# A key list for four engines and the transfers written anew, in a linear-attention and mixture-of-experts kernel

## The chip, the cores and the metric

One core of a Trainium2 chip runs one launch of the program. Its engines are TensorE (PE; its weight loads are shown as PEld), VectorE (DVE), ScalarE (ACT), GpSimd (POOL) and SyncE (SP), which issues nearly all transfers. The metric is the device time of one execution in microseconds, median of several runs.

## The reference

For each of 4 batches and 8 heads a complex state runs over 768 steps; then 3072 tokens go through two of eight experts each:

```python
mag = np.sqrt(a_re * a_re + a_im * a_im)
scale = np.minimum(mag, 0.999) / (mag + 1e-06)      # a_re_n, a_im_n = a * scale
for t in range(S):
    new_re = ar * S_re - ai * S_im
    new_im = ar * S_im + ai * S_re
    kv = np.einsum('bhd,bhe->bhde', k[:, :, t], v[:, :, t])
    S_re, S_im = (new_re + kv, new_im)
    y[:, :, t] = np.einsum('bhd,bhde->bhe', q[:, :, t], S_re)
logits = x @ w_gate
noisy_logits = logits + np.log1p(np.exp(x @ w_noise)) * noise
top2 = np.argpartition(-noisy_logits, 2, axis=1)[:, :2]       # softmax over the two
h = np.maximum(x[mask] @ w1[e], 0.0)
out[mask] += top2_w[mask, k, None] * (h @ w2[e])
```

## The kernel before, in words

The attention is cut into 24 units of 128 steps (n = 0 to 23; four units, one a batch, make a group g = n // 4; two units make a pair m). For a pair, `p1` (L330 on) turns the decay into logarithms (keys A1 to A4, D1 to D4), `p2a`, `p2carry` and `p2t` (L352 to L378) take the angle, add the carry of the group before (D5, which reads the tile `car`), sum along the steps on PE (P1, then A6, D7), and send the last row back to `car` by a transfer (S7). `p3` (L387) does the same for the magnitudes (P2, A9, A10, D9), sends a row to DRAM and back as a column (S5, S6). D10 and D11 turn q and k, PE transposes them (P3, P4; copied by A11, A12), forms scores (P5, masked by D12), the state (P6, D13) and the output (P7, A13; turned by P8, A14). After each group, the gate (keys G0 to G12; the last two groups in two parts, as G0.4 and G0.4b) picks experts and slots; POOL scatters the rows to `xs` in DRAM (`gate_scatter`, L566).

The experts follow: 72 matmuls of the first layer of expert 0, for the first 320 slots, are laid into the last attention units (P22.000 to P22.007, L764), then the second layer (P23.00 to P23.02, L833 and L839) and the first layer of expert 1. The remaining slots of expert 0 need every scatter: `xgb` is loaded from `xs` (L623) and turned on PE (`x_T`, L738). From there on the experts run one after another, outside the order given by hand.

What sets the order: a string of 1270 keys, `ORDER` (L208). A key's letter names the engine (A, D, P, S; G keys by the table `ON`, else DVE), and `key` (L289) collects the instructions made under it; most keys are one instruction, S6 (L399), S9 (L350), S14 and D25 are two, S10.0 four transfers. The keys' places also set where each step is emitted (`PLACE`, L862). The loop at L989 to L992 then chains, for each engine, the first instruction of a key behind the last one of the key before it. Of a key with two transfers, only the first has a floor and only the second holds what follows. Where no chain binds, the planner behind the tile framework places an instruction by its own costs. `PACE` (L527) holds back single scatters until a named ACT key is done.

Of the kernel before, what the change touches and what calls it, by code (L numbers as in the profile page):

```python
# [77 lines left out]
def kernel(  # L78
# [127 lines left out]
    phases, K = {}, {}  # L206

    ORDER = """  # L208
        A0.0 S1a.0 S1.1 S2a.0 S2.1 S1b.0 S2b.0 S3.0 A1a.0 A2a.0 A1b.1 A1a.1 D1a.0 A2b.1 A2a.1 D2a.0 S11.0
# [9 lines left out]
        D12a.1 S6.3 A6.7 P5b.1 D7.6 S1.5 A12.2 D7.7 P7a.1 S3.7 D8.3 P8.0 S7.5 A8.3 S12.5 P5a.2 D13.2 A7.3
        D11.3 P3.3 A14.0 D12b.1 A0.4 P2.4 D4.3 P5b.2 A9.4 D12a.2 P7b.1 A11.3 S5.4 D12b.2 P2.5 S2.5 A10.4 S4.4  # L220
        P4.3 A13.1 D9.4 S7.6 A9.5 S3.8 P2.6 A1.4 S6.4 D11.4 P7a.2 A10.5 S1.6 P7b.2 A12.3 D10.4 S5.5 P2.7 D9.5
        A13.2 P3.4 S4.5 A9.6 A2.4 S12.6 D10.5 P5a.3 A11.4 S3.9 D1.4 P5b.3 S7.7 A1.5 D12a.3 P4.4 A10.6 D12b.3
        A2.5 P7a.3 S6.5 D2.4 P7b.3 A12.4 P6.3 S2.6 D16.0 D1.5 S1.7 A13.3 P5a.4 S12.7 D13.3 A9.7 S5.6 A3.4 D2.5
        P8.1 P3.5 S3.10 A10.7 D3.4 S4.6 A3.5 P5b.4 D12a.4 A14.1 A4.4 D3.5 P7a.4 A11.5 D4.4 G0.0 A4.5 D11.5
        P6.4 S5.7 G1.0 S6.6 D9.6 A0.5 P8.2 P8.3 D12b.4 P4.5 S3.11 A14.2 D10.6 A5.4 S4.7 P7b.4 A14.3 S11.6 D5.4
        A5.5 S8.4 S12.8 D4.5 A12.5 P1.8 S2.7 P1.9 D5.5 A6.8 P3.6 A13.4 D7.8 S4.8 A6.9 D13.4 S6.7 G2.0 A11.6
        D7.9 S9.4 G3.0 D11.6 P1.10 A8.4 P1.11 S8.5 D8.4 A6.10 S11.7 P5a.5 A6.11 D7.10 S7.8 A7.4 P6.5 D7.11
        D8.5 P5b.5 A8.5 D9.7 P4.6 A7.5 D12a.5 A0.6 P2.8 D12b.5 D10.7 P2.9 A9.8 P7a.5 G4.0 D11.7 A10.8 G5.0
        A9.9 P7b.5 S5.8 G6a.0 D9.8 A12.6 S3.12 P2.10 G6b.0 D13.5 A13.5 P3.7 S6.8 G6c.0 G7.0 D10.8 A10.9 A1.6
        S5.9 P5a.6 G8a.0 D9.9 A9.10 P5b.6 A11.7 S3.13 G8b.0 D12a.6 S4.9 P2.11 A10.10 G8c.0 D12b.6 S9.5 A2.6  # L230
        P4.7 G8d.0 D9.10 P7a.6 A12.7 S6.9 G8f.0 D1.6 P7b.6 G9.0 S7.9 A1.7 G8e.0 S2.8 D2.6 P6.6 S5.10 A13.6
        S3.14 P5a.7 A2.7 G12a.0 G8g.0 D11.8 A9.11 P3.8 G12b.0 A10.11 D13.6 S1.8 A15.2 P8.4 D12a.7 S7.10 P8.5
        S6.10 A14.4 D1.7 P5b.7 A11.8 S4.10 G8h.0 G12c.0 P7a.7 D2.7 S5.11 A14.5 S3.15 A3.6 D12b.7 G10.0 S2.9
        P4.8 S7.11 A3.7 G12d.0 G11a.0 D3.6 P7b.7 A12.8 G12f.0 D10.9 P6.7 A13.7 S6.11 G12e.0 G12g.0 P8.6 G11b.0
        D3.7 P3.9 S13.0 A14.6 S3.16 D9.11 A4.6 S4.11 P5a.8 A11.9 D13.7 G0.1 D10.10 A4.7 P5b.8 D11.9 G1.1 P8.7
        D12a.8 P4.9 A14.7 D12b.8 A0.7 G2.1 D14.1 P6.8 G3.1 D15.4 D10.11 A5.6 P7a.8 A12.9 D5.6 P7b.8 A5.7
        D11.10 P1.12 A13.8 D5.7 P1.13 A6.12 P3.10 A6.13 D7.12 D7.13 P1.14 A11.10 D15.5 P1.15 D4.6 A6.14 P4.10
        A8.6 D8.6 D7.14 P5a.9 A6.15 D13.8 A7.6 P5b.9 D7.15 D12a.9 A12.10 P6.9 D8.7 P7a.9 A8.7 D12b.9 D4.7
        P5a.10 A7.7 P7b.9 D15.6 A0.8 G4.1 D11.11 P2.12 A13.9 D12a.10 P2.13 G5.1 A9.12 G6a.1 P3.11 D13.9 A10.12
        S5.12 G6b.1 G7.1 G6c.1 S4.12 D9.12 A9.13 P8.8 S7.12 A10.13 P6.10 S1.9 G8a.1 A11.11 D10.12 P5b.10 A1.8  # L240
        G8b.1 D9.13 P7a.10 A2.8 G8c.1 D12b.10 P4.11 A14.8 G8d.1 S6.12 D1.8 P2.14 A12.11 S3.17 P7b.10 G8f.1
        G8e.1 S5.13 G9.1 D15.7 A9.14 S2.10 G12a.1 P5a.11 G8g.1 S7.13 G12b.1 A13.10 D11.12 S4.13 A10.14 P8.9
        S1.10 D12a.11 P3.12 A14.9 G8h.1 G12c.1 D13.10 G10.1 P2.15 A11.12 S5.14 G11a.1 G12d.1 G11b.1 D16.1
# [5 lines left out]
        A6.18 P5b.13 A7.8 D7.18 D4.9 P7a.13 A6.19 A8.8 D7.19 P6.13 S8.9 D8.9 S8.8 A8.9 P5a.14 S6.15 D12b.13
        A7.9 P8.12 D11.15 S3.19 P5b.14 S7.16 A0.10 D10.15 S4.15 P2.16 G4.2 D12b.14 G5.2 P7b.13 A9.16 G6a.2  # L250
        A14.12 D12a.14 A10.16 P2.17 G6b.2 A13.13 G6c.2 S5.16 D9.16 P3.15 G7.2 S1.11 A9.17 A1.10 S7.17 G8a.2
        D13.13 P2.18 G8b.2 D10.16 A10.17 S6.16 P7a.14 A11.15 G8c.2 D9.17 S3.20 P7b.14 A9.18 S5.17 A2.10 G8d.2
        S9.9 P8.13 G8f.2 G8e.2 G9.2 A10.18 P4.15 G12a.2 S9.8 G8g.2 G12b.2 A14.13 G8h.2 G12c.2 D1.10 A13.14
        G10.2 P2.19 A12.15 S7.18 G12d.2 G11a.2 G12f.2 P6.14 S6.17 G12e.2 G12g.2 A1.11 D2.10 P3.16 S3.21 A9.19
        D11.16 A2.11 S5.18 P5a.15 S4.16 G11b.2 A11.16 D1.11 S7.19 P8.14 S12.9 A10.19 D12a.15 P4.16 A3.10 D2.11
        S5.19 P5b.15 A12.16 S6.18 D3.10 P7a.15 S13.2 A3.11 D12b.15 S3.22 P5a.16 A4.10 D3.11 P7b.15 A15.4
        D13.14 A4.11 D9.18 P6.15 A13.15 D10.17 A0.11 G0.3 S6.19 D4.10 P5b.16 A5.10 D13.15 P3.17 G1.3 D5.10
        A14.14 A5.11 G2.3 G3.3 D11.17 P1.20 A11.17 P1.21 D5.11 A6.20 P4.17 A6.21 D7.20 D7.21 P1.22 A12.17
        D16.2 D12b.16 P1.23 A6.22 D12a.16 P6.16 A8.10 D8.10 P5a.17 A6.23 D7.22 A7.10 D7.23 P8.15 D8.11 P5b.17
        A8.11 D9.19 A7.11 D14.3 D12b.17 A0.12 P2.20 D15.12 D4.11 P7a.16 A9.20 D10.18 P7b.16 A10.20 S5.20  # L260
        A14.15 S4.17 G4.3 D9.20 S3.23 P2.21 A13.16 P3.18 D11.18 A9.21 G5.3 A10.21 S5.21 P2.22 D12a.17 A11.18
        P2.23 G6a.3 D15.13 S14.00 A9.22 D9.21 P4.18 A10.22 S5.22 G6b.3 D13.16 P7a.17 G7.3 S12.10 A12.18 G6c.3
        S4.18 D9.22 P7b.17 A9.23 G8a.3 D10.19 A10.23 P6.17 S5.23 A13.17 G8b.3 D9.23 S20.00 P3.19 G8c.3 D11.19
        S12.11 P5a.18 A11.19 S6.20 G8d.3 P5b.18 D12a.18 S4.19 P4.19 G8f.3 D15.14 G9.3 G8e.3 G12a.3 P7a.18
        G8g.3 A12.19 G12b.3 D15.15 G8h.3 D13.17 G10.3 P21.000 S20.01 G11a.3 G12c.3 D12b.18 P5a.19 A23.000
        G12d.3 D23.000 P7b.18 G11b.3 S4.20 G12f.3 G12g.3 G12e.3 D10.20 P21.001 S6.21 A13.18 P6.18 A23.001
        D12a.19 A20.00 P5b.19 D23.001 D13.18 P21.002 D11.20 P6.19 A23.002 A20.01 S20.02 D23.002 P8.16 D10.21
# [960 lines left out]
```

## Time and profile before

| | us |
|---|---|
| median of 3 runs | 666.15 (665.39 to 666.69) |
| the profiled execution | 660.58 |
| its span, first to last instruction | 658.8 |
| busy in the span: PE, DVE, ACT, POOL | 625.9, 430.4, 328.0, 178.0 |

Times in the rows below count from the start of the span. A row of a timeline has a start, a duration, engine, line, operation, tiles and shapes, a count, and in brackets the idle time before it with what seems to have ended it.

### The profile page before, as it was taken

Reading aid. Unit: us, or ns where it says so; the run is one execution under the profiler, and the core shown is the slowest. Engines: PE = TensorE matmul, PEld = TensorE weight load, DVE = VectorE, ACT = ScalarE, POOL = GpSimd, SP = SyncE. Lnnn points to the kernel's source line nnn. Section 1 sums busy time; section 2 is a strip of 40 time slices with the busy share of each in tenths; the row PEclk is TensorE's granted clock in tenths of the full one; section 3 lists DMA queues with packets and bytes.
Section 4 is the critical chain, followed back from the end, with each engine's and each line's share of the span. In section 5 each row is a group of like instructions: output and inputs, shape, how many; then the busy total and the mean of one; then the engine's idle time right before and its main releaser. Section 6 shows DMA issues by size and latency. Waiting matters only on the chain.

```text
span 658.8 us, 13781 instructions
## 1 busy us (share of the span) xinstructions
PE 625.9 (95%) x5312; PEld 563.3 (86%) x5312; DVE 430.4 (65%) x957; ACT 328.0 (50%) x556; POOL 178.0 (27%) x185
## 2 busy tenths in 40 slices
...
GB/s 267 171 281 248 238 198 184 196 222 132 171 240 265 79 265 214 186 37 168 155 122 200 43 142 232 57 136 217 89 110 177 183 66 159 144 37 61 70 38 36
DMA packets 97049, 102.68 MB, mean 156 GB/s; under 512 B 60815, under 2 KB 78096, under 8 KB 96968
## 3 DMA queue, kind: packets, MB, share of 16 engines
...
q0 software_dynamic: 9344, 27.54, 11.7%
...
## 4 chain that ended last, share of the span: by engine, by line
PE 81%; ACT 7%; DVE 5%; DMA 3%; issue 2%; POOL 1%; SPq 0%; POOLq 0%; DVEq 0%; ACTq 0%
PE po L833 30%; PE ph L764 28%; PE ptr L415 4%; PE psc L426 3%; PE pY L477 2%; PE pY L479 2%; PE cum L366 2%; ACT t L297 2%; PE po L839 2%; PE psc L764 2%; PE cum L390 1%; PE pG L440 1%; PE cum L492 1%; ACT L296 1%; ACT ee L297 1%
## 5 line engine op out<-in xcount | busy, mean ns | idle before, releaser
L833 PE MATMUL po<-w2h,h 128*128 128x384 f32 x752 | 192.7, 335 | 0.0
L764 PE MATMUL ph<-x,w1h 128*128 128x512 f32 (+3 forms) x720 | 184.2, 344 | 0.0
L764 PEld LDWEIGHTS ph<-x,w1h 128*128 128x128 f32 x720 | 126.2, 189 | 14.5
L833 PEld LDWEIGHTS po<-w2h,h 128*128 128x128 f32 x752 | 135.9, 188 | 0.1
L833 PE MATMUL po<-w2l,h 128*128 128x384 f32 x376 | 125.7, 334 | 0.0
L764 PE MATMUL ph<-x,w1l 128*128 128x512 f32 (+3 forms) x360 | 124.0, 344 | 0.0
L848 POOL DMA_INDIRECT out_dram<-ao,ox x52 | 52.9, 1018 | 251.7 <-DVE ao L847 198.2
L777 DVE SCALAR_TENSOR_TENSOR h<-ph,h 128x256 fp32r<-128x256 f32 (+3 forms) x152 | 70.0, 482 | 65.8 <-ACT h L773 56.2
L571 POOL DMA_INDIRECT xs<-xr,sl x48 | 59.3, 1236 | 177.2 <-DVE t L342 92.9
L773 ACT ACTIVATE h<-ph 128x512 fp32r<-128x512 f32 (+2 forms) x112 | 55.9, 502 | 96.2 <-PE ph L764 95.8
L847 DVE SCALAR_TENSOR_TENSOR ao<-po,ex,ao 128x384 f32<-128x384 f32 (+1 forms) x42 | 25.8, 615 | 85.7 <-PE po L833 85.5
L764 PEld LDWEIGHTS ph<-x,w1l 128*128 128x128 f32 x360 | 67.9, 189 | 7.2
L833 PEld LDWEIGHTS po<-w2l,h 128*128 128x128 f32 x376 | 70.6, 188 | 0.1
L686 ACT CAST w2h<-raw 128x768 fp32r<-128x768 f32 x32 | 26.3, 833 | 82.1 <-PE po L833 72.3
L808 POOL DMA_INDIRECT ao<-out_dram,ox x49 | 55.6, 1134 | 35.5 <-DMA out_dram<-ao,ox 23.0
L744 ACT CAST x<-xt 128x512 fp32r<-128x512 f32 (+1 forms) x39 | 21.1, 547 | 53.8 <-DVE xt L743 52.6
L426 PEld LDWEIGHTS psc<-qT,kT 112*64 112x64 f32 x768 | 35.8, 137 | 5.8 <-issue 4.8
L426 PE MATMUL psc<-qT,kT 112*64 112x128 f32 (+1 forms) x768 | 40.6, 251 | 0.0
L687 DVE TENSOR_TENSOR w2l<-raw,w2h 128x768 fp32r<-128x768 f32 x32 | 30.2, 956 | 12.2 <-ACT w2h L686 9.9
L479 PE MATMUL pY<-am,v 128*48 128x128 f32 x384 | 35.9, 273 | 0.0
L428 DVE TENSOR_TENSOR am<-psc,mask 128x512 f32<-128x512 f32 x48 | 32.4, 683 | 2.5 <-PE psc L426 2.5
L477 PE MATMUL pY<-qT,z 112*48 112x128 f32 x320 | 31.8, 276 | 0.9 <-DVE z L462 0.9
...
## 6 DMA issues: line engine op xcount, KB each, us to landing
...
```

The lines of the kernel that those rows point to most:

```text
L426: key(f"P5{'ab'[half]}.{n}", nc.tensor.matmul(p[o:o + 64, j, s:], KT[n][:, h, s:s + 64], QT[n][:, h, s:], start=True, stop=True, skip_grou ...
L428: LAST['am'] = nc.vector.tensor_mul(AM[n][:, 4 * half:4 * half + 4, :].rearrange("p (i r) t -> p i r t", r=2), p.rearrange("p (i r) t -> p ...
L477: x = nc.tensor.matmul(o, Z[b][:, h, :], QT[n][:, h, :], start=True, stop=False, skip_group_check=True)
L479: x = nc.tensor.matmul(o, V[n][:, H + i if r else h, :], AM[n][:, h, :], start=not g, stop=True, skip_group_check=True)
L571: d = key(f"L{b}{kk}.{part(g, lo)}", nc.gpsimd.indirect_dma_start(out=xs, out_offset=bass.IndirectOffsetOnAxis(ap=sl[:, kk, b:b + 1], axis=0),
L687: d = key(f"D{name}", nc.vector.tensor_tensor(lo, raw_t, hi.bitcast(F32), op=OP.subtract))
L764: LAST['m'] = key(f"P22.{e}{w}{f}", nc.tensor.matmul(p[:, :c], W1[e, kk][i][:, f * 128:(f + 1) * 128], XW[w, kk][:, j, 0:c], start=(m == 0 ...
L773: key(f"A24.{e}{w}{f}", nc.scalar.activation(h[:, 0:c], p[:, :c], AF.Relu))
L777: LAST['h'] = key(f"D25.{e}{w}{f}", nc.vector.scalar_tensor_tensor(h[:, dst:dst + b - a], p[:, a:b], 0.0, h[:, hi:hi + b - a].bitcast(F32) ...
L808: nc.gpsimd.indirect_dma_start(out=ao[j][0:w, :], out_offset=None, in_=out, in_offset=bass.IndirectOffsetOnAxis(ap=OX[e][0:w, j:j + 1], ax ...
L833: LAST['po'] = key(f"P23.{e}{j}", nc.tensor.matmul(p[:, :DM], HT[w, f][i][:, o:o + 128], W2[f // 2][k2][:, f % 2, :], start=(m == 0), stop ...
L848: d = nc.gpsimd.indirect_dma_start(out=out, out_offset=bass.IndirectOffsetOnAxis(ap=OX[e][0:n, j:j + 1], axis=0), in_=a, in_offset=None, b ...
```

## The change

The whole string `ORDER` is replaced by another order of the same 1270 keys (on DVE 471, ACT 330, PE 277, SP 192 keys), `PACE` names other ACT keys, and the loop chains every instruction of every key, so that the second transfer of a key has a floor too and the first one a ceiling. No operation, tile, buffer or shape changes. Cut to what is spoken of below:

```diff
-    A0.0 S1a.0 S1.1 S2a.0 S2.1 S1b.0 S2b.0 S3.0 A1a.0 A2a.0 A1b.1 A1a.1 D1a.0 A2b.1 A2a.1 D2a.0 S11.0
-    A3a.0 S10.1 D1b.1 D3a.0 A1b.0 D2b.1 S10.0 A2b.0 D1a.1 A4a.0 D1b.0 A3b.1 D2b.0 D4a.0 S3.1 A3b.0 S2.2
-    P2.0 D3b.0 S4.0 D2a.1 A4b.0 S1.2 A3a.1 D4b.0 A9.0 D3a.1 P2.1 A10.0 D3b.1 A4a.1 D9.0 A4b.1 A9.1 D4b.1
-    A10.1 D4a.1 A0.1 S12.0 S5.0 A5a.0 S3.2 A5b.0 P1.0 A5b.1 S11.1 A5a.1 P1.1 S2.3 D6.0 D7.0 P1.2 D6.1 D7.1
-    A8.0 P1.3 S12.1 D6.2 S7.0 D8.0 S1.3 D7.2 A7.0 S5.1 D6.3 S6.0 D7.3 S3.3 A8.1 D8.1 D10.0 S11.2 A7.1 D9.1
-    A0.2 P2.2 S7.1 D11.0 S4.1 A1.2 P2.3 S12.2 D10.1 A9.2 D11.1 A2.2 P3.0 S3.4 A1.3 D1.2 A10.2 S11.3 A2.3
-    D2.2 P6.0 S1.4 S7.2 A11.0 D1.3 S6.1 A3.2 P4.0 D2.3 S5.2 S4.2 A9.3 D13.0 A3.3 S12.3 D3.2 P6.1 A12.0
-    S3.5 D3.3 A4.2 P5a.0 D13.1 A10.3 P3.1 D12a.0 A4.3 D9.2 P7a.0 A11.1 S4.3 P5b.0 S7.3 D9.3 A0.3 P4.1
...
-    P1.16 A11.14 G3.2 D5.9 P1.17 A6.16 D13.12 P4.14 A6.17 D7.16 D7.17 P1.18 A12.14 D8.8 P1.19 D12a.13
...
-    P3.20 D11.21 P7a.19 A11.20 D20.01 G0.4 A14.16 P4.20 D12b.19 G1.4 D20.00 P7b.19 A12.20 D10.22 G2.4
-    A20.02 P3.21 D16.3 G3.4 D11.22 P8.17 A11.21 P8.18 G4.4 D20.02 A13.19 P4.21 G5.4 A14.17 D10.23 P22.000
-    D11.23 S22.00 P22.001 A24.000 G6a.4 D25.000 P22.002 A24.001 D25.001 G6b.4 P8.19 G7.4 A24.002 A14.18
...
-    S20.11 G0.5 D14.5 G12c.4b D12b.23 P21.101 G1.5 P8.21 A23.101 G2.5 P7a.23 G3.5 G4.5 D23.101 G5.5 A14.21
-    G6a.5 P7b.23 G8h.4b G6b.5 G7.5 G6c.5 G12d.4b G8a.5 D16.4 G8b.5 G10.4b P21.102 G8c.5 G12e.4b A13.23
...
+    A0.0 S1a.0 S1.1 S2a.0 S2.1 S1b.0 S2b.0 S3.0 A1a.0 S4.0 S12.0 A2a.0 A1a.1 A1b.1 D1a.0 A2b.1 D2a.0 A2a.1
+    A3a.0 D1b.1 D3a.0 A1b.0 D2b.1 A2b.0 D1a.1 A4a.0 D1b.0 A3b.1 D2b.0 S3.1 D4a.0 A3b.0 S1.2 P2.0 D3b.0
+    S4.1 D2a.1 A4b.0 S11.0 A3a.1 D4b.0 A9.0 D3b.1 P2.1 A10.0 D3a.1 A4b.1 S3.2 D9.0 A4a.1 S2.2 A9.1 S5.0
+    A10.1 S1.3 A0.1 D9.1 S10.0 A5a.0 A5b.0 P1.0 D4b.1 A5b.1 D4a.1 A5a.1 P1.1 D6.0 D7.0 P1.2 S7.0 D6.1 S3.3
+    D7.1 S5.1 A8.0 S2.3 P1.3 D6.2 S11.1 D8.0 S6.0 D7.2 D6.3 A7.0 D7.3 A8.1 D8.1 S12.1 D10.0 A7.1 S3.4
+    D10.1 P3.0 A0.2 D11.0 A1.2 P2.2 A11.0 D11.1 S1.4 S4.2 P2.3 A2.2 S11.2 S7.1 P4.0 A1.3 D1.2 A9.2 P6.0
+    S3.5 D2.2 A2.3 S6.1 A12.0 D1.3 A3.2 P3.1 D2.3 A9.3 D3.2 A10.2 P5a.0 A3.3 S5.2 D13.0 S4.3 A4.2 D3.3
+    S7.2 P6.1 S11.3 A10.3 P5b.0 D9.2 S1.5 A4.3 S5.3 D12a.0 A11.1 S7.3 D12b.0 P7a.0 S3.6 A0.3 D9.3 P7b.0
...
+    G11b.1 D11.12 P1.16 A11.12 P1.17 D12a.11 A6.16 P4.12 D13.10 A5.9 D7.16 P6.11 D15.7 A6.17 D12b.11
...
+    A14.18 G12d.3 G8a.4 G8b.4 G8c.4 D10.22 P6.19 S4.22 A12.20 S12.11 G0.4b D11.21 P3.21 G1.4b A20.02
+    G12e.3 D11.22 G2.4b P8.19 A11.21 G3.4b D20.02 G10.3 P4.21 D10.23 P22.000 D11.23 S22.00 S6.23 P22.001
...
+    D12a.23 P5b.23 A13.22 P21.100 D12b.23 G0.5 A23.100 D22.02 P7a.23 G1.5 D23.100 S20.11 G2.5 P8.20 G3.5
+    P21.101 G4.5 D15.22 G5.5 P8.21 A23.101 G12d.4b G6a.5 G12e.4b G6b.5 P7b.23 D16.4 D23.101 G7.5 A14.20
+    G6c.5 G12f.4b G8a.5 A14.21 G12g.4b P8.22 G8b.5 A13.23 G8c.5 P21.102 G8d.5 A14.22 G8f.5 G8e.5 G0.5b
...
-        "L01.0": "A4.6", "L10.0": "A12.9", "L11.0": "A14.7", "L20.0": "A6.13", "L21.0": "A13.9", "L30.0":
...
+        "L01.0": "A14.5", "L10.0": "A6.12", "L11.0": "A14.6", "L20.0": "A6.14", "L21.0": "A9.12",
...
     for e in "ADPS":
         ks = [k for k in ORDER if (ON.get(k.split(".")[0], "D") if k[0] == "G" else k[0]) == e]
-        for a, b in zip(ks, ks[1:]):
-            tc.add_manual_dep(K[b][0].ins, K[a][-1].ins.name, after, reason="order at the start")
+        xs = [x.ins for k in ks for x in K[k]]
+        for a, b in zip(xs, xs[1:]):
+            tc.add_manual_dep(b, a.name, after, reason="order at the start")
```

## Rows read from the trace of the kernel before

**Rows 1.** Page, part 1: busy us, share of the span, instructions

```profile
PE 625.9 (95%) x5312; PEld 563.3 (86%) x5312; DVE 430.4 (65%) x957; ACT 328.0 (50%) x556; POOL 178.0 (27%) x185
```

**Rows 2.** Windows by stage: PE, PEld, DVE, ACT, POOL busy, clock, DMA share, GB/s

```profile
24.00:60.00 36.00, 28.98 (x353) 22.18 (x354) 32.27 (x46) 33.86 (x50) 0.00 (x0) 0.95 0.72 223
60.00:100.00 40.00, 38.81 (x610) 32.84 (x606) 39.47 (x87) 38.00 (x65) 0.28 (x1) 1.00 0.80 228
100.00:140.00 40.00, 39.94 (x668) 34.03 (x668) 39.25 (x89) 36.95 (x58) 16.07 (x15) 1.00 0.67 209
...
180.00:206.00 26.00, 25.70 (x387) 21.75 (x384) 25.75 (x68) 17.05 (x29) 10.98 (x7) 1.00 0.85 256
206.00:236.00 30.00, 30.00 (x366) 28.05 (x367) 19.56 (x76) 15.93 (x33) 9.11 (x9) 1.00 0.46 150
...
265.00:652.00 387.00, 386.20 (x2169) 363.83 (x2168) 194.33 (x342) 120.58 (x205) 105.28 (x98) 1.00 0.41 121
```

**Rows 3.** Timeline of DVE, 14 to 46 us

```profile
18.74 0.56 DVE L374 TENSOR_SCALAR tf<-cum 128x384 f32<-128x384 f32 x1 [3.36 <-PE cum L366]
...
25.54 0.95 DVE L395 TENSOR_TENSOR qk<-qk,ee 128x768 f32<-128x768 f32 x1
...
29.26 0.96 DVE L339 TENSOR_TENSOR t<-im,t 128x768 f32<-128x768 f32 x1 [0.16 <-ACT t L297]
...
44.39 0.95 DVE L361 SCALAR_TENSOR_TENSOR t<-car,t 1x768 f32<-1x768 f32 x1 [2.16 <-ACT tf L371]
```

**Rows 4.** Line L361 (D5): engine, count, duration min/median/max in ns, first and last

```profile
L361 DVEq EVENT_SEMAPHORE  x10: 21/50/3440, 38.5 to 170.1; - x10
```

**Rows 5.** Timeline of the transfer queue, 24 to 39 us

```profile
24.18 0.54 SPq L377 DMA_DIRECT2D car<-tf  x1
...
30.36 0.24 SPq L397 DMA_DIRECT2D es<-ee  x1
...
38.34 0.50 SPq L377 DMA_DIRECT2D car<-tf  x1
```

**Rows 6.** Waits of the transfer queue, 20 to 46 us: total, times, longest

```profile
SPq L397 <- ACT ee L297: 5.6, 1, 5.6
```

**Rows 7.** Timeline of ACT, 27.5 to 32 us

```profile
27.93 0.47 ACT L297 ACTIVATE ee<-cum 128x384 f32<-128x384 f32 x1
...
31.05 1.02 ACT L416 ACTIVATE qT<-ptr 112x1024 f32<-112x1024 f32 x1
```

**Rows 8.** Chain that ended last, 20 to 46 us: start, us, what

```profile
35.84 5.66 DMA v<-in_v_dram
```

**Rows 9.** Waits of DVE, 55 to 206 us

```profile
DVE qk L395 <- ACT ee L297: 0.6, 1, 0.6
...
DVE t L361 <- ACT t L297: 0.5, 2, 0.3
```

**Rows 10.** Waits of ACT, 55 to 134 us

```profile
ACT xr L493 <- PE cum L492: 2.4, 4, 0.9
```

**Rows 11.** Timeline of PE, 205 to 207 us and 235 to 241 us

```profile
205.75 1.09 PE L415 MATMUL ptr<-ident,kh 128*112 128x128 f32 x8 [0.30 <-ACT qT L416]
206.59 0.54 PE L764 MATMUL psc<-x,w1h 128*128 128x320 f32 x2
...
235.79 1.07 PE L504 MATMUL cum<-xT,wg 128*32 128x128 f32 x24
...
240.81 1.03 PE L504 MATMUL cum<-xT,wg 128*32 128x128 f32 x8
```

**Rows 12.** Timeline of POOL, 245 to 250 us

```profile
245.74 0.97 POOL L571 DMA_INDIRECT xs<-xr,sl  x1 [1.95 <-issue]
...
248.69 1.64 POOL L571 DMA_INDIRECT xs<-xr,sl  x1 [0.30 <-issue]
```

**Rows 13.** Chain that ended last, 240 to 266 us: start, us, what

```profile
259.31 4.67 DMA xgb<-xs
...
264.03 1.64 PE po L738 x12
```

More of the change, by code (lines that the diff above doesn't have):

```diff
@@ L219 @@
[L219 to L243, printed above, removed]
@@ L249 @@
[L249 to L267, printed above, removed]
-        P3.20 D11.21 P7a.19 A11.20 D20.01 G0.4 A14.16 P4.20 D12b.19 G1.4 D20.00 P7b.19 A12.20 D10.22 G2.4
@@ L274 @@
-        G7.4b G8a.4b G8h.4 G8b.4b D12a.21 A22.01 S22.02 P3.22 S14.10 G10.4 P22.006 A11.22 G11a.4 G12c.4 S6.23
-        G12d.4 D12b.21 A22.00 S4.22 G8c.4b G12e.4 P4.22 D22.00 P7a.21 A12.22 G8d.4b G8e.4b G12f.4 G8g.4b
-        P7b.21 G8f.4b D13.19 A24.006 S22.03 G9.4b D22.01 S13.4 P3.23 A13.21 G12a.4b D25.006 P22.007 G12g.4
-        S4.23 A11.23 P4.23 A24.007 D25.007 P5a.22 A12.23 S20.10 P5b.22 D12a.22 A22.03 P8.20 D12b.22 A22.02
-        P21.100 D22.03 P7a.22 A14.20 A23.100 D22.02 P7b.22 G12b.4b D23.100 P5a.23 A13.22 G11b.4 P5b.23 D12a.23
@@ new lines @@
+        P4.1 S4.4 D10.2 A5.2 S6.2 A13.0 D5.2 S2.4 A5.3 D11.2 S3.7 P1.4 A12.1 S11.4 P1.5 D5.3 A6.4 P3.2 A6.5
+        D7.4 D7.5 P1.6 S7.4 A11.2 S10.1 D4.2 P1.7 S12.2 A6.6 S2.5 P4.2 D13.1 A8.2 S6.3 D8.2 D7.6 A6.7 P5a.1
+        S3.8 A7.2 D7.7 P6.2 D12a.1 A12.2 P5b.1 D8.3 P7a.1 D13.2 A8.3 P5a.2 D12b.1 A7.3 D10.3 P5b.2 A0.4 P7b.1
+        D12a.2 P2.4 D4.3 A13.1 P3.3 A9.4 D12b.2 A10.4 S5.4 P2.5 D11.3 A11.3 S4.5 P7a.2 S7.5 D9.4 A1.4 P7b.2
+        S11.5 S3.9 P4.3 D11.4 A9.5 A13.2 P2.6 D10.4 A10.5 S6.4 A2.4 P6.3 D9.5 S4.6 A12.3 S7.6 P2.7 D1.4 S12.3
@@ new lines @@
+        A9.6 P5a.3 A1.5 D10.5 S2.6 P3.4 A9.7 S3.10 D12a.3 A2.5 S5.5 D2.4 P7a.3 A11.4 S1.6 P5b.3 S7.7 D1.5
+        A10.6 S12.4 P4.4 A3.4 S11.6 D12b.3 P8.0 A10.7 D2.5 A12.4 P8.1 D13.3 S5.6 P7b.3 A3.5 D3.4 S6.5 P3.5
+        A13.3 S4.7 D3.5 A4.4 P5a.4 S1.7 D11.5 P6.4 A14.0 A4.5 P5b.4 D12a.4 A14.1 G0.0 D4.4 A0.5 D12b.4 P8.2
+        S8.4 G1.0 S3.11 D9.6 A5.4 P7a.4 S2.7 A14.2 S12.5 D5.4 P7b.4 A5.5 D4.5 A11.5 P1.8 P1.9 D5.5 S8.5 A6.8
+        P4.5 S5.7 A13.4 D7.8 S6.6 A6.9 D13.4 P1.10 A12.5 D7.9 S3.12 S7.8 D16.0 P1.11 D8.4 A6.10 S9.5 D10.6
@@ new lines @@
+        A8.4 P5a.5 S4.8 D7.10 A6.11 S11.7 A7.4 G2.0 D7.11 P5b.5 G3.0 S7.9 D8.5 A8.5 P6.5 S3.13 D11.6 S6.7 A7.5
+        P8.3 D9.7 P3.6 A14.3 S9.4 A0.6 D12a.5 P2.8 G4.0 D11.7 P7a.5 G5.0 A11.6 G6a.0 D12b.5 P8.4 G6b.0 A9.8
+        D10.7 P4.6 A10.8 A14.4 G6c.0 P2.9 S5.8 D9.8 G7.0 A12.6 S7.10 P7b.5 S3.14 G8a.0 D10.8 A9.9 P5a.6 S6.8
+        A10.9 G8b.0 D13.5 A13.5 P2.10 G8c.0 S4.9 D12a.6 A1.6 S7.11 P2.11 G8d.0 A9.10 S5.9 D9.9 A2.6 S1.8 P6.6
+        G8e.0 A1.7 G8f.0 P3.7 D1.6 G9.0 A2.7 G8g.0 P5b.6 G12a.0 S2.8 D2.6 A11.7 S6.9 P7a.6 G12b.0 D1.7 A3.6
@@ new lines @@
+        S3.15 P4.7 G8h.0 A10.10 D12b.6 A9.11 G10.0 S5.10 G12c.0 D2.7 A12.7 P7b.6 S2.9 G11a.0 G12d.0 A3.7 D3.6
+        P5a.7 S1.9 A13.6 P5b.7 G12e.0 G12f.0 G11b.0 A10.11 D3.7 P3.8 A4.6 S6.10 G12g.0 D12a.7 P8.5 A4.7 S5.11
+        D12b.7 S4.10 P7a.7 A15.2 S13.0 A14.5 D11.8 A0.7 P7b.7 D4.6 P8.6 A13.7 D13.6 A5.6 G0.1 D9.10 A11.8
+        S6.11 D5.6 P6.7 A14.6 P4.8 D10.9 A5.7 D9.11 G1.1 A12.8 G2.1 P1.12 G3.1 D13.7 P1.13 A6.12 D5.7 P3.9
+        A6.13 D7.12 D11.9 A11.9 P1.14 D7.13 A6.14 P4.9 D4.7 A8.6 P1.15 D7.14 A12.9 D8.6 P5a.8 D10.10 A6.15
@@ new lines @@
+        P8.7 A7.6 D7.15 P6.8 D12a.8 A14.7 A8.7 P5a.9 D8.7 D14.1 P5b.8 A7.7 D11.10 A0.8 P2.12 D12a.9 D15.4
+        P2.13 G4.1 D10.11 G5.1 P5b.9 A1.8 G6a.1 P7a.8 D12b.8 A9.12 A2.8 G6b.1 S5.12 D15.5 P7b.8 S7.12 G6c.1
+        A10.12 D12b.9 G7.1 A9.13 P3.10 G8a.1 D1.8 A13.8 A10.13 P2.14 D13.8 A11.10 S2.10 G8b.1 P2.15 D2.8 S3.16
+        A9.14 S4.11 P4.10 A1.9 G8c.1 D15.6 D9.12 A3.8 P6.9 S7.13 A2.9 G8d.1 S6.12 P7a.9 D11.11 A12.10 S1.10
+        P7b.9 G8f.1 D1.9 S5.13 A9.15 P5a.10 A10.14 G8e.1 S2.11 G9.1 D2.9 A13.9 P8.8 S3.17 A10.15 P3.11 S7.14
```

54 lines of the change are left out of this document (39 added, 15 removed), and 12 rows, old and new, of the table PACE.

## The prediction, made before the result was known

> **What bounds the kernel now.** I read the page's busy shares first, then a table of windows by stage, then the timelines of the engines in the one stretch where the table shows idle time, then the waits and the chain at the end.
>
> The page gives PE 95% of the span [rows 1], so little seems left. The windows split that [rows 2]. From 265 us on PE is busy 386.20 of 387.00 us with weight loads at 363.83; the written order does not reach there, so this part keeps its length. From 206 to 236 us PE is busy 30.00 of 30.00 and its weight loads 28.05: PE-bound. Between 60 and 206 us PE also reads as full, but DVE does too (39.47 of 40.00, 39.25 of 40.00, 25.75 of 26.00), while PE's weight loads stand at 32.84, 34.03 and 21.75. From 24 to 60 us nothing is full: PE 28.98, DVE 32.27 and ACT 33.86 of 36.00. So until 206 us DVE sets the pace, an order can win what DVE waits, and the result comes down to when DVE has worked through the attention. A microsecond won there moves the whole rest, provided PE and the last scatters follow.
>
> **Part 1, the start (to 55 us).** DVE's timeline shows one hole after 24 us that counts: D5.3 at 44.39, 2.16 us after the operation before it [rows 3]. The row names ACT as the releaser. D5 has a separate waiting instruction on DVE's sequencer, and of the ten one took 3.44 us while the median is 0.05 us [rows 4]; ten is the number of D5s, and D5.3 is the only one with such a hole. What it needs beside ACT is `car`, sent by S7.3. That transfer was issued at 38.34 [rows 5], 6.0 us before D5.3 could start. It was late because of the queue: S7.1 was issued at 24.18, the next transfer, a store of `es`, at 30.36 [rows 5]; the queue stood 5.6 us for ACT's A10.2 [rows 6]. By the written order that store, S5.2, comes with seven keys between, behind S7.2. It could come early because S6.1's first transfer has no ceiling and the second no floor, so nothing held S5.2 down.
>
> In the new list every transfer is chained. S7.3 is the 39th S key instead of the 40th, but two output clears of 384 KB (S12.2, S12.3) and S10.1 go behind it, and S1.5 comes ahead. Walking the queue: S1.4 waits for A1.2, which on ACT ends at about 28.0 (its successor starts at 27.93 [rows 7]); six issues of about 0.5 us follow; S5.2 waits for A10.2, which is now behind A12.0 and A3.2. ACT's keys between the two table loads are the same set, and with the rows' durations A10.2 ends near 34.1; six more issues put S7.3 at 36.8. Landing takes between 2.9 us (the 288 KB v load issued at 35.84, shortly before it, took 5.66 us behind a full queue [rows 8]; I halve that for an emptier one) and the 6.0 us of now: 39.7 to 42.8.
>
> D5.3's turn on DVE: the same keys stand ahead of it as before, less D13.1 (a copy half as wide as the 0.95 us operations of rows 3: estimate 0.5 us). D9.1 moves from 25.54 into the hole of 3.36 us before 18.74 [rows 3], 0.95 us; but that is lost again, because D1.2 at 29.26 waits for ACT, and there A11.0 (1.02 us) now stands ahead of A2.2 where A9.2 (0.47 us) stood [rows 7]: D1.2 comes 0.55 us later. So D5.3 could start at 44.39 - 2.16 + 0.55 - 0.5 = 42.3, and its transfer is there between 39.7 and 42.8. I take no wait: the hole of 2.16 us is gone. D9.4's wait of 0.6 us [rows 9] goes too, since ACT's A10.4 gains the same 2 us and A14.0 (a copy) is now behind it. Sum at 55 us: -2.16 + 0.55 - 0.6 = **-2.2 us** (bounds -2.7, if the three small waits around D12a.0 and D5.2 go too, and -1.2, if the transfer is there at 42.8 plus the wait for P1.6).
>
> **Part 2, 55 to 206 us.** DVE waits 1.5 us in all there; the two largest are 0.6, counted already, and 0.5 in D5 [rows 9]. The new list moves the angle work of groups 3 and 4 forward: P1.16 passes 17 PE keys, D5.8 passes 15 DVE keys (six of them of the 0.95 us kind, in all 9.2 us by their rows' start-to-start times), but A5.8, which D5.8 reads, passes only 9 ACT keys (5.9 us, four of them of the 1.02 us kind). As ACT has run until now D5.8 would stand 3.3 us and hold everything behind it. ACT has idled in 55 to 134 us, though, the most of it 2.4 us in A14, waiting for PE [rows 10], and P8 is now later and ahead of need. If ACT closes that, some 1 us is left. Bounds 0 and +3.3; I take **+0.3** net of the 0.9 us of old waits, nearest to the rows that show all three engines full.
>
> **Part 3, the entry into the PE-bound part.** P22.000 began at 206.59, right after P4.21 had waited 0.30 us for ACT [rows 11]. Now G0.4b (1.03 us, as the same matmuls cost at 240.81 [rows 11]), G2.4b and P8.19 stand ahead of it, 1.6 us together. If PE is full, P22.000 is 1.6 us later; if it has the slack that the weight loads leave (21.75 of 26.00 [rows 2]), nothing. I take **+0.6**.
>
> The Trainium skill's page Perfetto Trace Analysis, section Identifying the Most-Contended Engine, says that TensorE's headroom is judged by its weight-load share and not by matmul occupancy, since matmuls are pipelined. By that rule this part would cost 0 and the sum below would be 0.6 us lower; by the matmul row (25.70 of 26.00) it would cost 1.6 us and the sum would be 1.0 us higher. No run has yet told them apart.
>
> **Part 4, the tail.** Between P22.000 (206.59) and G0.5 (235.79 [rows 11]) PE's keys are the same but for the three just moved ahead, P8.20 (now behind, 0.4 us) and G10.4b (now ahead). Walking PE's list against the two score buffers I find about 0.8 us of new stalls (P5b.20 waits for D25.002): 29.2 becomes 28.0. From G0.5 to the slots of the three tokens, G12g.5, D15.22 and G8a.5b are now ahead: +0.75. So the first scatter, at 245.74 [rows 12], comes 0.45 us nearer to P22.000. Behind it hang 18.3 us of scatters and load until PE starts on `xgb` at 264.03 [rows 12, 13], and that load itself is 4.67 us [rows 13]; PE, with 1.6 us less left to do, waits there. S20.12 (512 KB) now runs beside these scatters; they took between 0.97 and 1.64 us each [rows 12], so I add **+0.3** (bounds 0 and 4 x 0.67 = 2.7). Tail: -0.45 + 0.3 = **-0.15**.
>
> **Sum:** -2.2 + 0.3 + 0.6 - 0.15 = -1.45 us. The profiled execution then takes 660.58 - 1.45 = 659.1 us with a span of 657.3; the median of the runs, 666.15, becomes **664.7**.
>
> **Rivals.**
> *No change: the gain at the start is eaten.* S7.3 lands at 42.8 and PE takes its 1.6 us: -1.2 + 0.3 + 1.6 - 0.15 = +0.55, between 665.3 and 667.3. For it speaks that PE reads as full from 60 us on; against it its weight loads.
> *Slower: ACT holds DVE in the middle.* Place: D5.8 and the D7.16 to D7.19 behind it, which read A6.16 to A6.19. The price is the 3.3 us of part 2. It decides once ACT keeps more than about 0.5 us of its idle time before A5.8; then PE, whose P1.16 comes 17 keys earlier and waits for the same D5.8 in order, does not catch up by 206 us and its 1.6 us count too: -2.2 + 3.3 + 1.0 + 0.6 = +2.7: 668.9.
> *More is won.* All waits of DVE in 55 to 206 us go, no stall comes, PE absorbs its 1.6 us: -2.7 - 0.9 - 0.45 = -4.0: 662.1.
> *The chain does not do what it says:* the transfers would keep floating and S7.3 stay near 38; then the new list alone acts, close to the first rival.
>
> **Chances.** Forecast (-3 to -0.8) 0.42; no change 0.26; slower 0.23; more 0.09. A measurement of this kernel tells about 0.2% (1.3 us) from nothing. Of the forecast's share about 0.39 lies beyond that: faster 0.48, same 0.29, slower 0.23. The likeliest case alone spans 663.1 to 665.5. The range that leaves out two in ten reaches from the larger gain to the slower case: 661.5 to 669.5.
>
> **What would show it.** Right: the queue's wait for ACT near 24 to 30 us splits into one until about 28 and one until about 34; S7.3 issued before 37; no hole of 2 us before a D5 near 42; DVE's keys near 55 us some 2 us earlier; P22.000 between 205 and 206; POOL's last group of scatters 1 to 2 us earlier, and PE idle 1 to 2 us before its matmuls on `xgb`. Wrong: a wait of over 1 us before a D5 or an L372 between 100 and 145 us, or P22.000 later than 206.6. A change of the length behind 265 us would contradict the first paragraph.

## The result, and the profile after

The changed kernel took 671.03 us (median of 4 runs, 669.39 to 672.74) against 665.77 us of the kernel before on the same chip: 1.0073 of it, 95% interval 1.0055 to 1.0091. It is slower by 5.3 us where 1.5 us less was forecast. On another chip, in a later run, the same kernel is *faster*: 658.27 against 660.9 us, 0.9968 (0.9957 to 0.9980). Both results hold, and most of what follows is why.

The profiled execution of the changed kernel took 669.39 us (span 667.6 us). First the page, part 1, which answers [rows 1]:

```profile
PE 629.9 (94%) x5312; PEld 564.8 (85%) x5312; DVE 430.1 (64%) x957; ACT 326.5 (49%) x556; POOL 172.6 (26%) x185
```

The windows by stage (PE, PEld, DVE, ACT, POOL busy, clock, DMA share, GB/s), beside [rows 2]:

```profile
24.00:60.00 36.00, 29.49 (x390) 23.11 (x392) 33.77 (x48) 35.02 (x54) 0.00 (x0) 0.95 0.79 238
60.00:100.00 40.00, 38.89 (x589) 31.21 (x586) 38.38 (x86) 38.67 (x65) 2.50 (x2) 1.00 0.87 240
100.00:140.00 40.00, 38.74 (x516) 30.67 (x516) 37.98 (x87) 35.30 (x58) 17.40 (x14) 1.00 0.51 161
...
180.00:206.00 26.00, 26.00 (x395) 22.26 (x394) 25.35 (x69) 17.66 (x34) 0.84 (x2) 1.00 0.84 265
206.00:236.00 30.00, 26.52 (x301) 24.01 (x300) 19.45 (x76) 12.51 (x23) 8.07 (x8) 0.94 0.48 162
...
265.00:652.00 387.00, 386.62 (x2178) 363.77 (x2177) 198.56 (x366) 123.71 (x213) 105.21 (x100) 1.00 0.42 124
```

From 24 to 60 us DVE does 1.5 us more than in the first trace of before: the start goes the way that was forecast. From 60 us on DVE idles in every window (38.38, 37.98), and in 206 to 236 us PE, which was busy 30.00 of 30.00, is down to 26.52 at a granted clock of 0.94. The part behind 265 us keeps its length.

The start, beside [rows 3 to 5]: issues of `car` and `es` on the transfer queue, D5.2 and D5.3 on DVE, and D5's own wait.

```profile
34.85 0.23 SPq L397 DMA_DIRECT2D es<-ee  x1
...
38.50 0.51 SPq L377 DMA_DIRECT2D car<-tf  x1
```

```profile
40.69 0.94 DVE L361 SCALAR_TENSOR_TENSOR t<-car,t 1x768 f32<-1x768 f32 x1 [0.27 <-ACT t L297]
42.44 0.94 DVE L361 SCALAR_TENSOR_TENSOR t<-car,t 1x768 f32<-1x768 f32 x1
```

```profile
L361 DVEq EVENT_SEMAPHORE  x10: 21/50/797, 37.6 to 167.3; - x10
```

D5.3 starts at 42.44 with no idle time ahead of it, and the longest of the ten waits is 797 ns instead of 3440.

Then the place of the largest loss, the timeline of 213 to 222 us, all engines:

```profile
215.19 0.89 PE L426 MATMUL psc<-qT,kT 112*64 112x128 f32 x16
...
216.25 0.97 POOL L571 DMA_INDIRECT xs<-xr,sl  x1 [0.30 <-issue]
...
216.55 0.89 PE L426 MATMUL psc<-qT,kT 112*64 112x128 f32 x16 [0.47 <-issue]
...
217.52 0.97 POOL L571 DMA_INDIRECT xs<-xr,sl  x1 [0.30 <-issue]
219.48 1.29 DVE L428 TENSOR_TENSOR am<-psc,mask 128x512 f32<-128x512 f32 x2 [3.08 <-remote]
...
220.22 0.57 PE L479 MATMUL pY<-am,v 128*48 128x128 f32 x4 [2.57 <-DVE am L428]
```

D12a.20 (219.48) needs nothing but P5a.20, whose matmuls end at 215.19 + 0.89 = 216.08. It starts 3.4 us later, and "remote" means that the profile could not name who released it: the semaphore record of P5a.20 is stamped 219.46, 3.4 us behind the modelled end of its last matmul, and that of P5b.20 0.15 us after it. PE then waits for DVE, and its clock falls. I call this a late signal. The Trainium skill, page Perfetto Trace Analysis, section Tensor Engine Instruction (MATMUL, LD_WEIGHTS), says that PE's end in a profile is an estimate from the instruction's size and that the signal goes out once PSUM has acknowledged; so a PE row can look finished while nobody has been told. The two stamps here agree with it.

Another one of the same kind: D11.10 idles 1.13 us; its release is stamped 110.39, 0.59 us behind the end of the last matmul ahead of it, and behind a scatter again. Taken in order, the stamp is that of P6.8, the row at 107.67 (end 108.60), so 1.8 us late.

```profile
107.67 0.93 PE L440 MATMUL pG<-v,kh 128*48 128x48 f32 x32
...
108.76 1.05 POOL L571 DMA_INDIRECT xs<-xr,sl  x1 [0.30 <-issue]
...
110.42 0.96 DVE L405 TENSOR_TENSOR kh<-qk,tr 128x768 f32<-128x768 f32 x1 [1.13 <-PE psc L426]
```

Between 60 and 265 us the semaphore records show late signals (over 0.3 us) in nine clusters, every one within 2.1 us of a scatter's start, and of PE alone: no recorded signal of DVE or ACT is late. Just there records are missing, though: in the whole trace 93 of 1302 of DVE and ACT and about 20 of 511 of PE, all less than 2 us behind the start of an indirect transfer, so whether those signals came late can't be told. The first trace of the kernel before has none of either.

### The profile page after: what moved, and what is told of

Its sections match the earlier page's. It is cut to its first block, busy times and chain, and to the rows that moved or that the text cites. A ratio compares the mean times of both kernels' runs of the same rounds, so it can differ in the third digit from the quotient of the medians.

```text
span 667.6 us, 13778 instructions
## 1 busy us (share of the span) xinstructions
PE 629.9 (94%) x5312; PEld 564.8 (85%) x5312; DVE 430.1 (64%) x957; ACT 326.5 (49%) x556; POOL 172.6 (26%) x185
## 4 chain that ended last, share of the span: by engine, by line
PE 81%; ACT 7%; DVE 6%; DMA 2%; issue 2%; another core or an unknown queue 0%; SPq 0%; POOL 0%; POOLq 0%; DVEq 0%; ACTq 0%
PE po L833 29%; PE ph L764 28%; PE ptr L415 4%; PE psc L426 3%; PE pY L477 2%; ACT t L297 2%; PE pY L479 2%; PE cum L366 2%; PE po L839 2%; DMA out_dram<-ao,ox 2%; PE psc L764 2%; PE pG L440 2%; PE cum L390 1%; PE cum L492 1%; PE cum L504 1%
## 5 line engine op out<-in xcount | busy, mean ns | idle before, releaser
L571 POOL DMA_INDIRECT xs<-xr,sl x48 | 57.6, 1199 | 186.4 <-DMA im<-in_a_dram 88.0
```

The source lines that it names most:

```text
L571: d = key(f"L{b}{kk}.{part(g, lo)}", nc.gpsimd.indirect_dma_start(out=xs, out_offset=bass.IndirectOffsetOnAxis(ap=sl[:, kk, b:b + 1], axis=0),
```

## The experiments

The chips on which the runs fell are of two kinds, told apart by the kernel before, which ran beside each: 665.4 to 666.3 us on three of them ("with late signals", like the chip of the result), 660.8 and 660.9 us on two ("without"). The runs on each chip were made in one stretch of time, so a chip can't be told from its hour. A ratio is always to the kernel before on the same chip.

**t1_tie, t2_list, h1_start, h3_oldtail: which part costs?** On one chip with late signals.

```diff
# t1_tie: list and PACE of before, only the loop changed
+        xs = [x.ins for k in ks for x in K[k]]
# t2_list: list and PACE of after, the loop as before
-        for a, b in zip(xs, xs[1:]):
+        for a, b in zip(ks, ks[1:]):
# h1_start: ORDER = new list up to D9.4 + the remaining keys in the old order
# h3_oldtail: ORDER = new list up to P22.000 + the remaining keys in the old order
```

> The old list and the old PACE, only the loop is the new one, so that both transfers of a key are tied. If the tying by itself is what costs (transfers that used to float to a free moment now stand in a row behind late ones), this takes 669 to 671 us, most of the way from 665.8 to 671.0. If the new list is what costs, the tying changes little: 664.5 to 667, and since S5.2's store can no longer overtake S7.2 the hole of 2.16 us before D5.3 should shrink by about 1 us.

Measured 664.84 us, 0.9996 (0.9981 to 1.0011): tying costs nothing.

> The new list and the new PACE with the old loop. If the list costs: 669.5 to 672.5, as the changed kernel. If the tying costs: 665 to 667, as before.

Measured 669.99 us, 1.0066 (1.0041 to 1.0091): on such a chip the loss comes with the list (and its `PACE`), not with the loop.

> New list up to D9.4 (about 55 us), behind it the remaining keys in the old list's order, old PACE, new loop. The trace of the changed kernel has DVE 1.7 us ahead at 60 us. Theory 'the start is a gain and the rest loses it': 663.5 to 665, faster than before by 1 to 2 us. Theory 'a gain at the start is lost anyway, because PE or the scatters cannot follow': 665.5 to 667. Theory 'the start itself breeds the later stalls': 669 to 671.

Measured 664.85 us, 0.9993 (0.9980 to 1.0006) and, as h1_again and h1_third on two more chips of this kind, 0.9992 (0.9981 to 1.0002) and 0.9990 (0.9981 to 0.9999). The start alone neither costs nor gains much here.

> New list up to P22.000 (about 210 us) with the new PACE of groups 0 to 2, behind it the remaining keys in the old list's order with the old PACE. In the profiled execution of the changed kernel 4.4 us went between P5b.20 and P22.003, behind P22.000, and 4.2 us ahead of it. Theory 'the tail's order costs': 666 to 667.5. Theory 'what costs lies before P22.000': 669.5 to 671.5. Theory 'late completions of PE that come with any order': the 4.4 us do not vanish but turn up elsewhere, 668 to 672, and the trace shows waits of DVE or ACT for a PE that had long finished.

Measured 672.2 us, 1.0092 (1.0070 to 1.0114). The old tail does not help: the loss lies between D9.4 and P22.000, or moves wherever the tail is. In its trace D12a.20's wait is shorter, and one of 4.99 us follows at 222.57: D12b.20 starts 5.6 us behind the end of P5b.20 (217.00), and in between the trace has a single signal of PE, stamped 222.55. Six scatters stand there in a row, 1.28 us apart, the last from 221.53 on.

**b0_again, t3_pace, x1_after, x1_before: is it the scatters?** On a chip without late signals, as it turned out.

```diff
# b0_again: the kernel before. t3_pace: the changed kernel with the PACE of before
# x1_*: 32 plain transfers for the 24 scatters of groups 0 to 2, to fixed rows instead of the slots
-                d = key(..., nc.gpsimd.indirect_dma_start(out=xs, out_offset=..., in_=XR[g][:, lo + b, :], ...))
+                d = key(..., nc.gpsimd.dma_start(x3[i % 8, i // 8 * 128:i // 8 * 128 + 128], XR[g][:, lo + b, :]))
```

> The kernel before, unchanged, for a second trace of it. Its first trace was of an execution of 660.58 us, 5 us under its own median, and shows no wait for a PE that had finished; the old list with the new loop shows some near 197, 203 and 234 us. If the first trace was of a luckier execution than the timed ones, this one takes 664 to 666 us and shows waits of DVE or ACT near the same places, 4 to 5 us in all, each behind a scatter. If those waits come from the tying, it takes 660 to 661 us and shows none.

Measured 660.66 us: as its first trace, with one late signal of 0.30 us. So the first trace was no lucky execution: it most likely came from a chip without late signals, while the three times beside it (665.39 to 666.69) came from one with them. The record doesn't name the chip of that trace; on the three chips with late signals none of 57 timed runs of the kernel before is below 663.71.

> The new list and the new loop with the old PACE: the scatters of group 3 hang on A23.001 to A24.000 again, 198 to 213 us, and no longer on A14.19 to A24.006, 214 to 231 us. Theory 'scatters hold back PE's signals': D12a.20's wait of 3.1 us behind P5a.20 goes and comes up smaller near 200 us, 667.5 to 670 us. Theory 'it is the place of P5a.20 and D12a.20 in the list': the wait stays, 670 to 672 us.

Measured 658.43 us, 0.9965 (0.9952 to 0.9978): faster than before, with no late signal in the trace. Neither theory had this.

> The changed kernel, its 24 indirect scatters of groups 0 to 2 replaced by 32 plain transfers of the same rows from the same queue at the same points, so the slots are wrong. Theory 'scatters hold back PE's signals': between 60 and 190 us no wait for a PE that had finished is left (five in the changed kernel's trace, 3.5 us of DVE's idle time), P22.000 comes at 207 to 208.5 instead of 210.8, and the time is 667.5 to 669. Theory 'the list is what costs': P22.000 stays at 210 to 211 and the time at 670 to 672.

Measured 659.21 us, 0.9977 (0.9962 to 0.9992).

> The same replacement in the kernel before. Theory 'scatters hold back PE's signals': it gains little, since its late signals fall behind the scatters of group 3 and later, 664 to 666, so the gap between the two lists shrinks from 5.3 to about 3 us. Theory 'the list is what costs': the gap stays at 5 to 6 us.

Measured 660.23 us, 0.9993 (0.9980 to 1.0005). Without late signals there was nothing for these two to remove: they say only that plain transfers are no faster by themselves.

**a1_again, t3_again, x1_again, h2_newtail: the changed kernel beside its variants.** Another chip without late signals.

> The changed kernel, unchanged, beside the kernel before on whatever chip this is. The runs so far fall into two kinds: on one chip the kernel before takes 665.4 us and PE's completion signals come up to 3.4 us late behind scatters, on another it takes 660.8 us and none does. Theory 'late signals': where before takes 660 to 661 this one takes 657.5 to 659.5, faster, with no wait for a finished PE and P22.000 at 205 to 206; where before takes 665 to 666 it takes 670 to 672 with the late signals at the same places as in its first trace. Theory 'the new PACE costs': 662 to 667 where before takes 660.8, and 671 where it takes 665.5. Theory 'the list costs': 1.005 to 1.01 of before on either kind of chip.

Measured 658.27 us, 0.9968 (0.9957 to 0.9980). The same stretch of its trace as above, with the scatters at the same places:

```profile
209.19 0.89 PE L426 MATMUL psc<-qT,kT 112*64 112x128 f32 x16
...
210.14 0.68 DVE L428 TENSOR_TENSOR am<-psc,mask 128x512 f32<-128x512 f32 x1
210.25 0.97 POOL L571 DMA_INDIRECT xs<-xr,sl  x1 [0.30 <-issue]
...
211.29 0.69 DVE L428 TENSOR_TENSOR am<-psc,mask 128x512 f32<-128x512 f32 x1 [0.47 <-PE psc L426]
```

P5a.20 ends at 210.08 and D12a.20 starts at 210.14. Its windows, against [rows 2]:

```profile
60.00:100.00 40.00, 39.74 (x583) 31.83 (x582) 39.36 (x87) 39.61 (x66) 4.00 (x3) 1.00 0.84 240
100.00:140.00 40.00, 39.65 (x605) 32.69 (x605) 39.81 (x91) 37.51 (x62) 17.82 (x15) 1.00 0.52 166
...
206.00:236.00 30.00, 29.70 (x391) 27.46 (x391) 21.35 (x89) 15.44 (x30) 13.90 (x14) 1.00 0.56 201
```

DVE is as full as it was before: the waits in the middle of the changed kernel's first trace are not the list's alone, they need a chip with late signals.

> New list, new loop, old PACE, once more beside the changed kernel on one chip. Theory 'late signals': the same as the changed kernel within 0.3 per cent on either kind of chip, since the slots of group 3 (G12g.3) come later than either PACE. Theory 'the new PACE costs': faster than the changed kernel by 5 us or more on either kind.

Measured 659.02 us, 0.9969 (0.9957 to 0.9982): the new PACE costs nothing on such a chip.

> The changed kernel with plain transfers for the indirect scatters of groups 0 to 2 (slots wrong), once more beside the changed kernel itself. Theory 'late signals come from the indirect scatters': on a chip that shows them, none is left between 60 and 190 us, P22.000 comes at 207 to 208.5 instead of 210.8, and the time is 2 to 3.5 us below the changed kernel's; on a chip that shows none, the same as the changed kernel within 0.3 per cent. Theory 'they come from any transfer of the queue': no difference on either.

Measured 658.85 us, 0.9971 (0.9961 to 0.9981).

> Old list up to P22.000, from there the remaining keys in the new list's order with the new PACE of groups 3 and later, new loop. It has the old places of the first 32 scatters and the new tail. Without late signals: the tail's gain alone, 0.5 to 1.5 us below before (PE reaches its matmuls on xgb 0.5 to 1.5 us earlier). With late signals: the wait behind P5a.20 of the changed kernel's tail comes up here too if it is bound to the tail's order, 667 to 669; if it is bound to the four scatters that stand beside it, which come 10 us earlier here, 664 to 666.

Measured 660.74 us, 0.9997 (0.9987 to 1.0007). P22.000 is late, and the shorter way from there to `xgb` (56.09 us against 57.75) gives most of that back:

```profile
207.80 0.65 PE L492 MATMUL cum<-ident,xT 128*128 128x128 f32 x4
208.21 0.54 PE L764 MATMUL psc<-x,w1h 128*128 128x320 f32 x2
```

against 205.56 in b0_again, whose PE keys up to there are the same but for G0.4b, G2.4b and P8.19 (the row at 207.80 is P8.19). DVE and ACT have some G keys more ahead too, and the loop is the new one. Of the +2.65 us 0.48 are there at P4.21 already (205.20 against 204.72); the other 2.17 are the three keys (1.6 us by the prediction's rows) and a wait of 0.34 us for ACT ahead of G2.4b.

**x2_after: no indirect scatter at all.** The replacement of x1, for all 48, one for one. The plain transfers read no slots, and the load of `xgb` no longer waits for the last of them. This run fell on a chip with late signals.

> The changed kernel with all 48 indirect scatters replaced by plain transfers of the same rows from the same queue at the same points, so the slots are wrong. On a chip with late signals (before near 665.5): theory 'the indirect scatters hold PE's signals back': no wait for a finished PE is left and it takes 656 to 660 us, where the changed kernel was 5.3 us above before; theory 'any transfer of that queue does': the late signals stay and it takes 664 to 671. On a chip without them (before near 660.8): 656 to 659, within 0.3 per cent of the changed kernel there.

Measured 658.57 us where the kernel before took 666.27: 0.9885 (0.9867 to 0.9903). That is the time that the changed kernel has on a chip without late signals. The same stretch:

```profile
210.22 0.89 PE L426 MATMUL psc<-qT,kT 112*64 112x128 f32 x16
...
210.97 1.07 POOL L573 DMA_DIRECT2D xs<-xr  x2 [0.53 <-ACT h L777]
...
211.18 0.68 DVE L428 TENSOR_TENSOR am<-psc,mask 128x512 f32<-128x512 f32 x1
```

No late signal is left before 359 us; the seven behind it stand within 2.3 us of the indirect transfers of the output, which this kernel still has. So PE's signals are held back where the transfers are indirect, and not where plain ones come from the same queue. That these also start more freely is not what made up the time: PE reaches P22.000 at 205.88 and `xgb` at 261.46, no earlier than in a1_again, which has the scatters (204.85 and 260.68).

**p1_g3: the four scatters moved away from P5a.20.** A chip with late signals.

```diff
-        "L01.3": "A14.19", "L10.3": "A24.002", "L11.3": "A24.002", "L20.3": "A12.21", ...
+        "L00.3": "A24.003", "L01.3": "A24.003", "L10.3": "A24.004", "L11.3": "A13.20", "L20.3": "A24.005", ...
```

> The changed kernel, only the PACE of group 3's eight scatters is moved: the first four to A24.003, A24.003, A24.004 and A13.20 (they stood beside P22.002, P5a.20 and P5b.20), the other four spread up to A24.006. On a chip with late signals: if the wait of 3.1 us before D12a.20 is bound to the scatters beside P5a.20 it goes, and the time falls from 1.0073 of before to 1.000 to 1.004; if it is bound to the list's order there, 1.006 to 1.009. On a chip without them: as the changed kernel there, 0.996 to 0.998.

Measured 670.29 us, 1.0064 (1.0050 to 1.0079), not to be told from 1.0073. The wait left D12a.20 and went with the scatters:

```profile
214.69 0.68 DVE L428 TENSOR_TENSOR am<-psc,mask 128x512 f32<-128x512 f32 x1
...
222.01 0.98 POOL L571 DMA_INDIRECT xs<-xr,sl  x1 [0.30 <-issue]
...
223.29 0.97 POOL L571 DMA_INDIRECT xs<-xr,sl  x1 [0.30 <-issue]
225.23 0.69 DVE L428 TENSOR_TENSOR am<-psc,mask 128x512 f32<-128x512 f32 x1 [2.85 <-remote]
225.32 1.02 ACT L416 ACTIVATE qT<-ptr 112x1024 f32<-112x1024 f32 x1 [3.13 <-remote]
```

D12a.20 (214.69) is free, D12a.21 (225.23) now waits 2.85 us; the matmuls of P5a.21 that it reads had ended at 221.21, 4.0 us before. No version was found that beats both kernels on both kinds of chip: the new list is the fastest without late signals, and with them only t1_tie and h1_start, which were run on no other, are not slower than before (x2_after aside, whose rows go to the wrong slots).

## Why the prediction was wrong, point by point

The milestones of the traces, all PE, in us from the start of the span (starts of the rows of P22.000, P23.00, the first matmuls on `xgb`, and the span):

```
                                        P22.000  P23.00   xgb     span
before, first trace (without)            206.59  242.36  264.03  658.8
b0_again (without)                       205.56  241.31  263.31  659.0
a1_again, the changed kernel (without)   204.85  239.81  260.68  656.3
t1_tie, the old list (with)              207.66  245.56  267.43  663.0
the changed kernel, first trace (with)   210.84  251.35  272.34  667.6
x2_after (with, no scatters)             205.88  240.85  261.46  657.2
```

**The step that failed** is the last of the sum: "The profiled execution then takes 660.58 - 1.45 = 659.1 us with a span of 657.3; the median of the runs, 666.15, becomes 664.7." The first half is close to what a1_again shows (656.3 us of span, 658.27 us). The second half took the 5.57 us between the one profiled execution and the median for a constant that the change does not touch. It was the price of late signals that the profiled execution did not have, and the new list raises that price: with them the old list takes 4.9 us more (665.77 - 660.9), the new one 12.8 us more (671.03 - 658.27). That the signals are the price is shown for the new list, by x2_after; for the old one, which was not run without scatters on such a chip, it is argued from the same waits in t1_tie. No rival had this mechanism. That the page's time lay 0.7% under the fastest timed run was the one sign of it ahead of the result.

**Part 1** was right in place and close in size. D5.3's hole is gone, the queue's wait split in two, D1.2 waits 1.56 us as A11.0 stands ahead, and up to 60 us DVE has done 51.81 us of work in a1_again against 50.41 in b0_again, 1.4 us more. One such pair tells it to about 1 us only: the first trace of before, the same program as b0_again, has 49.29. S7.3 was issued at 38.50 (37.91 in a1_again), not before 37; it did no harm, because D5.3's turn came no earlier than 42.4.

**Part 2**, the rival in which ACT holds DVE at D5.8, did not happen in either trace: no wait stands before D5.8. The waits that the first trace of after shows there (0.97 us before D5.6, 0.84 before D7.18) go in a1_again, where L372 waits 0.2 us in all from 55 to 206 us.

**Part 3** cost about 1.1 us, not the 0.6 that I took. DVE's busy time in 60 to 180 and in 180 to 206 us, a1_again first, then b0_again:

```profile
60.00:180.00 120.00, 118.34 (x272) 1.00 0.67 193
180.00:206.00 26.00, 24.64 (x65) 1.00 0.93 282
```

```profile
60.00:180.00 120.00, 118.00 (x270) 1.00 0.68 195
180.00:206.00 26.00, 25.72 (x67) 1.00 0.88 271
```

Up to 180 us the new list gains another 0.3 us, so parts 1 and 2 gave 1.4 + 0.3 = 1.7 us (1.9 were forecast). Then DVE loses 1.1 us, and the waits that appear there are for PE but for 0.2 us. What is left, 0.7 us, is the lead with which a1_again comes to P22.000. These 1.1 us are not all proven to be the three keys', which a1_again spreads over 200 to 203 us; in h2_newtail, where they stand right ahead of P22.000, they cost 2.2 us with the wait among them. By the weight-load share, the rule of the page Perfetto Trace Analysis of the Trainium skill that the prediction weighed against the matmul row, they would have cost nothing; neither trace bears that out, and the matmul row (25.70 of 26.00) was nearer.

**Part 4** is the term that was mis-sized: -0.15 forecast, -1.9 measured. From P22.000 to `xgb` it takes 57.75 us in b0_again and 55.83 in a1_again. The rows of b0_again and a1_again:

```profile
205.56 0.54 PE L764 MATMUL psc<-x,w1h 128*128 128x320 f32 x2
...
244.68 0.97 POOL L571 DMA_INDIRECT xs<-xr,sl  x1 [1.93 <-issue]
...
263.31 1.64 PE L738 MATMUL po<-ident,xgb 128*128 128x128 f32 x12 [0.73 <-DMA xgb<-xs]
```

```profile
204.85 0.54 PE L764 MATMUL psc<-x,w1h 128*128 128x320 f32 x2
...
242.58 1.85 POOL L571 DMA_INDIRECT xs<-xr,sl  x1 [3.09 <-issue]
...
260.68 1.46 PEld L738 LDWEIGHTS po<-ident,xgb 128*128 128x128 f32 x12 [0.35 <-DMA xgb<-xs]
260.68 1.65 PE L738 MATMUL po<-ident,xgb 128*128 128x128 f32 x12
```

The first of the last eight scatters comes 37.7 us behind P22.000 instead of 39.1: 1.4 us nearer where 0.45 was forecast, mainly because PE went from P22.000 to G0.5 in 27.3 us and not 28.0 (of the 0.8 us of new stalls 0.3 came). The eight take as long as before (10.57 us from the first start to the last, against 10.50), and the load of `xgb` takes 4.5 us from issue to landing instead of 5.0, which the sum did not have. That load still releases PE's weight load (the 0.35 us in the last fence), but it lands just as PE is through: the last matmul ahead ends at 260.60, the load at 260.64. So the wait of 1 or 2 us that I expected did not come, and PE's own way, 1.3 us shorter than in b0_again, was not held up. The sum is -0.7 - 1.9 = -2.6 us, as measured (658.27 - 660.9). That this lies within the forecast's own span (-3 to -0.8) is in part luck: part 3 and part 4 were missed in opposite directions. (The upper end of that span is 666.15 - 0.8 = 665.35 us, where the prediction has 665.5.)

**Open:** why the new list pays 12.8 us for about as many late signals (26 in its first trace) as cost the old one 4.9 (22 in t1_tie). Against the same kernel without them it loses 6.0 us by P22.000 and 5.5 us from there to P23.00, the old list 2.1 and 2.2 (rows b0_again and t1_tie). In the old list they fall where DVE has other work until 196 us: from 60 to 180 us DVE is busy 118.04 us in t1_tie and 118.00 in b0_again, while in the new list it falls from 118.34 in a1_again to 113.54; p1_g3 shows that moving four scatters moves the loss and doesn't lessen it. That the new list leaves less room everywhere is likely but only argued. Open too is what in an indirect transfer holds PE's signals back (it reads slots, and it keeps GpSimd busy 0.97 us and more where a plain one takes 0.54), whether the chip or the hour makes the difference, and whether the recording, which loses records in the same windows, has a part in it.
